# Sinkhorn attention and a gated layer on one core: a new order for the first hundred calls and the later ones, and zero products cut in pieces elsewhere

## The chip, the cores and the metric

The kernel runs on one core of a Trainium2 chip. The metric is device time in microseconds (us) of one execution, as the median of several runs; lower is better. The engines are TensorE (PE in the profile, its weight loads PEld), VectorE (DVE), ScalarE (ACT), GpSimd (POOL) and SyncE (SP, which here issues transfers).

## The reference, cut to what matters

```python
# q, k, v: 4 batches, 8 heads, 768 positions, 64 wide; sort_net: 4, 8, 8, 8
P = sort_net
for _ in range(5):                              # the balancing
    P = exp(P - max(P, -1)); P = P / sum(P, -1); P = P / sum(P, -2)
k_sorted = einsum('bhij,bhjcd->bhicd', P, k_blocks)   # 8 blocks of 96 positions
v_sorted = einsum('bhij,bhjcd->bhicd', P, v_blocks)
scores = q_block @ k_sorted_block.T / 8               # 96 x 96 for each block and head
attn = softmax(scores)
x = (attn @ v_sorted_block)                           # rearranged to 3072 tokens x 512
h = x @ w_in                                          # 512 -> 2048
out = (h * cos(h)) @ w_out                            # 2048 -> 512, float32
```

## The kernel before, in words

The 3072 tokens are worked in 8 chunks of 384 tokens. Chunk n is half of one batch: 4 tiles u of 96 positions, each with all 8 heads. A chunk passes through these calls, each a small function of the kernel that records instructions on a fixed engine:

- the sorted keys, `kp`/`ks`/`kg` (products on PE into tile `ks`) with their evictions `kpe`/`kse`/`kge` into `kTs`; the sorted values, `v0`/`vb`/`vg`/`vgT` (products into `vs`) with the evictions `v0e`/`vbe`/`vge` into `vS` or `pair`;
- `S n u` or `T n u`: the scores of a tile (tile `sc`); `M`: their row maximum on DVE (`mx`); `X`: the subtraction on DVE (`s`); `E`: the exponential on ACT (`p_buf`);
- the transposed weights, either on PE with an eviction (`TP`, tile `pps`, and `TE`, tile `pT`) or by a transposing transfer on SP's queue (`TD`);
- `AV`: weights times values on PE (`av`); `N`: a reciprocal `r` and a product `xn` on DVE;
- the transposed x, by PE and an eviction (`XP`, tile `xps`, and `XE`, tile `xT`) or by a transfer (`XD`);
- the up layer, `U` (PE, tile `h`), `C` (the cosine on ACT, tile `c`), `G` (the product on DVE, tile `gg`); for chunk 0 `U4`, `C4`, `G4` do it in halves of the tokens;
- the down layer, `D n ts q` (four products of 512 columns on PE into tile `o`), `O` (the eviction) and `W` (the write).

Which call stands where is not left to a scheduler. `PLAN` is a text of some 790 lines, one call each, and a loop at the kernel's end runs them in that order, so each engine gets its instructions in the order of the plan. Within an engine nothing overtakes. Tiles in PSUM come from two pools, `big` (three buffers; the letter B in a call) and `acc` (two buffers; the letter c); a call that needs a buffer waits until an earlier tile has been evicted. The letters A and V in an eviction say ACT or DVE. What the plan does on PE in one stretch is covered by the evictions on ACT and DVE in the next, so the chunks are interleaved: the keys and scores of chunk n+1 stand between the layers of chunk n.

The program begins with the transfers of q, k and v, the five balancing rounds (small DVE and ACT work on 32 partitions) and, beside them on PE, **zero products**: `keep_warm(times, t, cols)` (L1051 to L1062) multiplies a zero tile `warm` into a tile that is overwritten later. They are called in the balancing (tile `idle`), and inside the plan by `kp` and `v0` (as many as the last argument, 512 columns each) and by `TP` and `AV` of chunk 0 (256 columns each). A counter `pieces` allows a number of them to be cut into pieces: before, each call is cut in up to four until 70 cuts are used up, which the balancing does alone.

The balanced matrix `sorted_by` is followed on PE by `block` (tile `bl`), and on DVE by `spread` (tiles `bd` and `bdv`), which the plan's `kp` and `v0` read. `v0 3`, `v0 1`, `v0 2` and `v0 0` read v as it landed (`kv`); `v0 4` to `v0 7` read `vperm`, which `vp 32` makes from it on POOL in two copies (L993).

## Time and profile before

| what | value |
|---|---|
| median of 3 runs | 236.35 us (236.2 to 237.87) |
| the profiled execution, its own time | 236.52 us |
| its span from first to last instruction | 234.7 us |
| PE busy | 227.7 us, 97% of the span |
| DVE busy | 175.2 us, 75% |
| ACT busy | 149.1 us, 64% |
| POOL busy | 93.7 us, 40% |

The profile is of one execution; the 1.8 us between its time and its span lie around the instructions. Positions are us from the first instruction. In a timeline row stand start, duration, engine, line, operation, output and inputs, shape and count, and in brackets the idle time before it and what ended it. Products on PE are pipelined and their ends are modelled, so PE rows overlap: the time that a group costs is the distance to the start of the next. A row of the chain that ended last has start, duration and what was done; there the parts do not overlap.

### The profile page before, as it was taken

The page shows a single profiled execution, that of the slowest core. Times are in us where ns is not written, and L with a number is a line of the kernel's source. Part 1 is how long each engine was busy: PE and PEld are TensorE (multiplying, and loading weights), DVE is VectorE, ACT ScalarE, POOL GpSimd, SP SyncE. Part 2 cuts the span into 40 slices and gives each one's busy share as a digit, 9 for nine tenths or more (in the row PEclk, how much of TensorE's full clock was granted, in tenths as well). Part 3 has the DMA queues.
Part 4 walks back from the last instruction along what each step waited for, and adds up shares of the span by engine and source line. Part 5 has one row for each costly group of instructions (what it writes and reads, how often), then busy time and mean ns, then how long its engine had stood idle before and what let it go on. Part 6 is the DMA issues. An engine that isn't in the chain of part 4 may idle for free.

```text
span 234.7 us, 5734 instructions
## 1 busy us (share of the span) xinstructions
PE 227.7 (97%) x2380; PEld 151.0 (64%) x2380; DVE 175.2 (75%) x291; ACT 149.1 (64%) x198; POOL 93.7 (40%) x117
## 2 busy tenths in 40 slices
PE   8898999999999999999999999999999999999994
PEld 8766799657765566655666558655555596456553
DVE  5757987798898776897778977899487879455530
ACT  3365976657869859883788747666667376526511
POOL 7659998596990095972709000800000000000000
PEclk9999999999999999999999999999999999999999
DMA  5999999796699779996999668953943650341003
GB/s 63 223 195 207 204 207 226 128 216 164 134 102 179 167 138 168 99 218 152 127 158 95 86 104 148 210 83 68 162 159 64 82 175 3 66 125 47 0 0 134
DMA packets 66841, 31.01 MB, mean 132 GB/s; under 512 B 55552, under 2 KB 62336, under 8 KB 66560
## 3 DMA queue, kind: packets, MB, share of 16 engines
q0 software_dynamic: 24048, 13.64, 43.6%
q1 hardware_dynamic: 42480, 16.83, 34.1%
q8 instruction: 18, 0.29, 0.5%
q10 hardware_dynamic: 288, 0.20, 0.3%
q14 instruction: 7, 0.06, 0.1%
HBM read 27.27 MB, written 6.29 MB: 143 GB/s over the span
## 4 chain that ended last, share of the span: by engine, by line
PE 84%; DMA 7%; ACT 3%; POOL 3%; issue 1%; DVE 1%; DVEq 0%; POOLq 0%
PE o L1544 32%; PE h L1499 30%; DMA kv<-in_v_dram 6%; PE h L1522 5%; PE av L1430 3%; POOL vperm L993 2%; PE sc L1320 2%; PE ks L1201 2%; PE xps L1469 2%; PE o L1638 2%; DMA kv<-p_buf 1%; PE vs L1257 1%; PE pps L1406 1%; PE vs L1292 1%; PE sc L1347 1%
## 5 line engine op out<-in xcount | busy, mean ns | idle before, releaser
L1544 PE MATMUL o<-w_out_t,gg 128*128 128x512 bf16 x368 | 87.2, 379 | 0.0
L1499 PE MATMUL h<-xT,w_in_t 128*128 128x384 bf16 (+1 forms) x516 | 78.2, 305 | 0.0
L1511 DVE TENSOR_TENSOR gg<-c,h 128x768 bf16<-128x768 f32 x56 | 53.0, 949 | 19.0 <-ACT c L1505 18.9
L1505 ACT ACTIVATE c<-h,half_pi 128x768 f32<-128x768 f32 x56 | 50.4, 901 | 22.0 <-PE h L1499 20.7
L1499 PEld LDWEIGHTS <-w_in_t 128*128 128x128 bf16 x516 | 47.1, 98 | 22.4 <-DVE xT L1072 0.2
L1544 PEld LDWEIGHTS <-gg 128*128 128x128 bf16 x368 | 33.3, 98 | 33.7 <-DVE gg L1511 0.6
L1379 ACT ACTIVATE p_buf<-s 96x768 bf16<-96x768 f32 x32 | 26.4, 841 | 12.1 <-DVE s L1375 8.0
L1361 DVE TENSOR_REDUCE mx<-sc 96x8 f32<-96x768 f32 (+1 forms) x41 | 31.5, 772 | 3.3 <-PE sc L1333 1.4
L993 POOL COPY vperm<-kv 64x1536 bf16<-64x1536 bf16 (+1 forms) x10 | 28.1, 2853 | 2.5 <-DMA kv<-in_v_dram 2.5
L1375 DVE TENSOR_TENSOR s<-sc,mx 96x384 f32<-96x384 f32 (+1 forms) x33 | 24.1, 733 | 1.2
L1447 DVE TENSOR_TENSOR xn<-av,r 96x512 bf16<-96x512 f32 x32 | 22.0, 687 | 1.1
L943 POOL DMA_DIRECT2D kv<-in_q_dram x24 | 16.0, 681 | 0.8 <-issue 0.5
L1446 DVE RECIPROCAL r<-av 96x8 f32<-96x8 f32 x32 | 6.3, 198 | 8.1 <-PE av L1430 8.0
L1070 ACT CAST kTs<-ks 128x512 bf16<-128x512 f32 (+1 forms) x18 | 11.0, 632 | 2.2 <-PE ks L1201 2.2
L1070 ACT COPY xT<-xps 128x384 bf16<-128x384 bf16 x10 | 4.8, 476 | 11.3 <-PE xps L1469 11.3
L943 POOL DMA_DIRECT2D q_mem<-in_q_dram x16 | 10.7, 685 | 2.8 <-DMA kv<-in_v_dram 2.4
L1070 ACT COPY kv<-o 128x512 f32<-128x512 f32 (+2 forms) x10 | 5.3, 529 | 9.6 <-PE o L1544 7.0
L1059 PEld LDWEIGHTS <-warm 128*128 128x128 bf16 x116 | 9.8, 119 | 2.3 <-DVE half_pi L1042 1.0
L1522 PE MATMUL h<-xT,w_in_t 128*128 128x192 bf16 x128 | 11.1, 246 | 0.0
L1059 PE MATMUL idle<-warm 128*128 128x128 bf16 (+2 forms) x99 | 9.7, 273 | 1.3 <-DVE half_pi L1042 1.0
L1522 PEld LDWEIGHTS <-w_in_t 128*128 128x128 bf16 x128 | 10.4, 98 | 0.0
L1567 POOL CAST held<-q_turned 96x1 f32<-96x1 bf16 x2 | 0.4, 182 | 24.4 <-DMA q_turned<-q_mem 17.0
(120 smaller groups left out, 276.4 us busy)
## 6 DMA issues: line engine op xcount, KB each, us to landing
out_dram<-kv SPq DMA_DIRECT2D x12, 256.0 KB, 2.5
out_dram<-o_s SPq DMA_DIRECT2D x10, 256.0 KB, 3.3
w_in_t<-in_moe_w_in_dram POOLq DMA_DIRECT2D x4, 512.0 KB, 12.4
w_out_t<-in_moe_w_out_dram POOLq DMA_DIRECT2D x4, 512.0 KB, 11.6
kv<-in_k_dram POOLq DMA_DIRECT2D x2, 768.0 KB, 10.0
kv<-in_v_dram POOLq DMA_DIRECT2D x2, 768.0 KB, 13.6
pair<-in_k_dram POOLq DMA_DIRECT2D x2, 768.0 KB, 10.3
kv<-in_v_dram POOLq DMA_DIRECT2D x6, 256.0 KB, 6.1
```

The source lines that it names most:

```text
L943: nc.gpsimd.dma_start(out=q_heads[:, i, :, e], in_=src[:, ih * IC + i, :, e])
L993: nc.gpsimd.tensor_copy(dst, src)
L1070: eng.copy(dst, src)
L1361: nc.vector.reduce_max(mx[:], s_view(n, u, hp), axis=AX.XY if n < 2 else AX.X)
L1375: nc.vector.tensor_tensor(s, sc, mx.to_broadcast(list(s.shape)), op=ALU.subtract)
L1379: nc.scalar.activation(p[:, :, :blk], s_t.pop((n, u)).rearrange("p e h c -> p (e h) c"), AF.Exp, scale=scale)
L1447: nc.vector.tensor_tensor(xn.rearrange("p h e d -> p e h d")[:, e], avv[:, :, :, :D], r[:, e].to_broadcast([blk, e.stop - e.start, H2, D]) ...
L1499: nc.tensor.matmul(o[:, f2, x * w:(x + 1) * w], w_in_t[:, kk, f * 128:(f + 1) * 128], xT[n][:, kk, x * w:(x + 1) * w], start=(kk == 0), st ...
L1505: nc.scalar.activation(c[:], ps["h", n, fp][:, :, :TC], AF.Sin, bias=half_pi[:, 0:1])
L1511: nc.vector.tensor_tensor(gt[n, fp // 2][:, f:f + 2], ps.pop(("c", n, fp))[:], ps.pop(("h", n, fp))[:, :, :TC], op=ALU.mult)
L1522: nc.tensor.matmul(o[:, part, f2 * w:(f2 + 1) * w], w_in_t[:, kk, f * 128:(f + 1) * 128], xT[0][:, kk, h * w:(h + 1) * w], start=(kk == 0) ...
L1544: nc.tensor.matmul(out_ps[n, ts][:], gt[n, q][:, f % 4, ts * 128:(ts + 1) * 128], w_out_t[:, f, :], start=(f == 0), stop=(f == FC - 1))
```

## The change

Three things are changed. The plan's first hundred or so calls come in another order, and two zero products leave them (those of `kp 2` and of `v0 4`). `keep_warm` cuts differently: a product of 512 columns in up to five and one of 256 in three, 18 cuts for the balancing and 52 for the plan, of which the plan uses 44. And from chunk 0's down layer on, calls are moved by one to a few places all through the plan; `S 6 0` becomes `T 6 0` (the same scores by products of 64 rows), `U 2 6` and `U 7 6` do half of their work in products of 192 columns in place of 384, and `TE 1 3` and `vbe 4` go from DVE to ACT, `XE 2 2` from ACT to DVE.

```diff
-MORE = 70
+MORE = 18,52
 PLAN = """\
-vp 32
 kp 0 B 1
 spv
-kp 2 B 1
+kp 2 B
+kp 1 B
+vp 32
 kpe 0 A
-kp 1 B
+v0 3 c 1
+v0 4 B
+kpe 1 A
 kpe 2 V
-v0 3 c 1
-kpe 1 A
+S 0 0 B
+v0e 3 V
 v0 1 c 1
-v0e 3 V
-S 0 0 B
+v0e 4 A
+S 0 1 B
 v0e 1 A
-v0 4 B 1
...
     AV 2 1
     N 2 1
     kg 3 B
+O 1 1 o A
+X 3 0
+D 1 2 0
...
-T 4 0 B
-vge 0 8 A
-AV 3 1
 hp 3 3
 Lq 5
+T 4 0 B
 D 2 1 1
 M 4 0
 X 4 0
+AV 3 1
 N 3 1
+vge 0 8 A
...
-    pieces = [MORE]
+    pieces = [MORE[0]]
...
-            n = 1 + min(3, pieces[0])
+            n = min(1 + pieces[0], max(3, cols // 102))
...
+    pieces[0] = MORE[1]
     for line in PLAN.split("\n"):
```

After the change, lines from L1052 on have a number that is one higher. The first place is PE after the sorted keys: before, the last products of `v0 1` (from `kv`) are followed by the scores `S 0 0`.

```order
L1257 LDWEIGHTS kv
L1257 MATMUL vs<-bdv,kv 128x128
L1257 LDWEIGHTS kv
L1257 MATMUL vs<-bdv,kv 128x64
L1333 LDWEIGHTS q_turned_94
L1333 MATMUL sc<-kTs,q_turned_94 128x64
```

After the change the last products of `v0 3` are followed by `v0 4`, which reads `vperm`, and the scores come behind it.

```order
L1258 MATMUL vs<-bdv,kv 128x128
L1258 LDWEIGHTS kv
L1258 MATMUL vs<-bdv,kv 128x64
L1258 LDWEIGHTS vperm
L1258 MATMUL vs<-bdv,vperm 128x128
```

So PE's scores of tile 0 now stand behind a product that waits for POOL's first copy into `vperm`.

The second place is DVE at the end of chunk 1's down layer, where chunk 2's tiles are finished; numbers tell the tiles apart. Before, `M 3 0` and `X 3 0` (the rows with `sc_1694`) come ahead of `N 2 1` (those with `av_1713`).

```order
L1446 RECIPROCAL r_1666<-av_1650 96x8
L1447 TENSOR_TENSOR xn_1667<-av_1650,r_1666 96x2x4x64
L1361 TENSOR_REDUCE mx_1707<-sc_1694 96x8
L1375 TENSOR_TENSOR s_1709<-sc_1694,mx_1707 96x768
L1446 RECIPROCAL r_1722<-av_1713 96x8
L1447 TENSOR_TENSOR xn_1723<-av_1713,r_1722 96x2x4x64
```

After the change the same six are in this order (`sc_1683` and `av_1699` are the same two tiles).

```order
L1447 RECIPROCAL r_1661<-av_1649 96x8
L1448 TENSOR_TENSOR xn_1662<-av_1649,r_1661 96x2x4x64
L1362 TENSOR_REDUCE mx_1697<-sc_1683 96x8
L1447 RECIPROCAL r_1708<-av_1699 96x8
L1448 TENSOR_TENSOR xn_1709<-av_1699,r_1708 96x2x4x64
L1376 TENSOR_TENSOR s_1719<-sc_1683,mx_1697 96x768
```

`N 2 1` now stands ahead of `X 3 0`, one long DVE instruction earlier.

The third place is PE in chunk 2's down layer, at `T 4 0` (the last scores there are of tile `sc`) and `AV 3 1` (from `kv`, where a transfer puts the transposed weights). Before, one follows the other.

```order
L1347 MATMUL sc<-kTs,q_turned_94 128x96
L1347 LDWEIGHTS q_turned_94
L1347 MATMUL sc<-kTs,q_turned_94 128x96
L1430 LDWEIGHTS kv
L1430 MATMUL av<-vS,kv 128x65
```

After the change `D 2 1 1`, four products of 512 columns, stands between them; its last two are shown.

```order
L1545 LDWEIGHTS gg
L1545 MATMUL o<-w_out_t,gg 128x512
L1545 LDWEIGHTS gg
L1545 MATMUL o<-w_out_t,gg 128x512
L1431 LDWEIGHTS kv
L1431 MATMUL av<-vS,kv 128x65
```

`AV 3 1` thus comes four products later behind the same scores. In the same stretch `AV 3 0` and `N 3 0` moved to the stretch's beginning, so that on DVE `N 3 0` now stands ahead of `M 3 3` and `X 3 3`.

## The prediction

> **What bounds the kernel now.** I read the busy times first (the page's, then by stretches), then the waits of PE, then the chain that ended last and timelines of single stretches.

> ```profile
> PE 227.7 (97%) x2380; PEld 151.0 (64%) x2380; DVE 175.2 (75%) x291; ACT 149.1 (64%) x198; POOL 93.7 (40%) x117
> 20.00:25.00 5.00, 4.41 (x92) 3.57 (x92) 4.16 (x6) 3.92 (x7) 4.94 (x7) 1.00 1.29 203
> 180.00:200.00 20.00, 20.00 (x193) 14.23 (x191) 15.80 (x24) 11.94 (x15) 0.00 (x0) 1.00 0.45 92
> ```

> PE is busy for 97% of the span; DVE, the next, has a quarter of its time free. By stretches of the span (columns: length, then PE, PEld, DVE, ACT and POOL busy) PE has gaps early (4.41 of 5 us from 20 to 25) and none late (20.00 of 20). A new order of calls changes no amount of real work. It can only take away waits of PE, so the waits are the whole purse:

> ```profile
> PE vs L1257 <- POOL vperm L993: 0.6, 1, 0.6
> PE qps L1136 <- DMA q_mem<-in_q_dram: 0.6, 1, 0.6
> PE av L1430 <- DMA kv<-p_buf: 0.3, 1, 0.3
> PE pps L1406 <- ACT p_buf L1379: 0.2, 1, 0.2
> ```

> The wait for the queries (`q_mem`) stands in the balancing, whose order the change leaves alone, and so do the rows left out here. What remains is 0.6 for `vperm`, 0.3 for a transfer and 0.2 for an exponential, 1.1 us or 0.5% of the time, and stalls that are too short for this view. That caps a gain. A loss has no such cap.

> **The early stage.** The chain there, up to the first product of the up layer:

> ```profile
> 15.74 5.55 POOL vperm L993 x2
> 25.42 0.87 PE vs L1257 x8
> 26.32 0.58 ACT vS L1070
> 27.69 0.56 PE pps L1406 x8
> 30.87 2.68 PE h L1522 x32
> ```

> POOL copies v as soon as it has landed, PE works through values and scores until `v0 0` (25.42), whose eviction on ACT stands ahead of the exponential of tile 3, which the transposes at 27.69 wait for. The question is when `v0 0` is done in the new order. These rows of PE's and POOL's timelines give it:

> ```profile
> 17.63 0.39 PE L1059 MATMUL vs<-warm 128*128 128x512 bf16 x1
> 19.02 0.39 PE L1059 MATMUL vs<-warm 128*128 128x512 bf16 x1
> 19.34 0.59 PE L1257 MATMUL vs<-bdv,vperm 64*128 64x128 bf16 x8
> 21.34 0.20 PE L1257 MATMUL vs<-bdv,vperm 64*128 64x64 bf16 x1 [0.59 <-POOL vperm L993]
> 26.21 0.28 PE L1059 MATMUL pps<-warm 128*128 128x256 bf16 x1
> 15.74 2.78 POOL L993 COPY vperm<-kv 64x1536 bf16<-64x1536 bf16 x1 [2.10 <-DMA kv<-in_v_dram]
> ```

> From 17.63 (the zero product ahead of `v0 1`) to 26.21 (behind `v0 0`) PE takes 8.58 us. In it are the wait of 0.59 and the zero product of `v0 4`, 19.34 - 19.02 = 0.32, which goes. The new order does the same work (the `TP 0 0` that stood in its middle is still ahead of `v0 0`), but it starts with `v0 4`, which needs the first copy: 15.74 + 2.78 = 18.52, and 0.05 to see it (as 21.34 stands behind 15.74 + 5.55). Without wait and zero product the rest is 8.58 - 0.59 - 0.32 = 7.67, so `v0 0` ends at 18.57 + 7.67 = 26.24, against 26.21. The wait at 21.34 goes, and a longer one takes its place: PE now reaches `v0 4` at about 17.3 (before, `v0 3` ended at 17.63, and the 0.32 for the zero product of `kp 2` ahead of it are gone) and stands until 18.57. **This stage gives nothing.**

> The cuts add a little. Eight products of 384 columns take 1.30 us in the chain, and 32 of 192 take 2.68 (at 30.87):

> ```profile
> 88.51 1.30 PE h L1499 x8
> ```

> That is 163 ns against twice 84, so one more product costs some 5 ns. Of the 44 cuts in the plan some 24 stand behind `v0 4` and ahead of the up layer, 0.12 us; the others are covered by the wait for `vperm`. In the balancing a cut more or less is covered by the wait for the queries (the 0.6 above). The two `U` that are split add four products each, 0.04 together.

> What could make the stage better: tile 1's scores now come before `v0 5`, so DVE no longer stands between `X 0 0` and `M 0 1`:

> ```profile
> 21.81 0.95 DVE L1361 TENSOR_REDUCE mx<-sc 96x8 f32<-96x768 f32 x1 [0.74 <-PE sc L1333]
> ```

> It loses 0.3 at the start (`S 0 0` waits for POOL too) and saves the 0.74, some 0.4 us. If the DVE chain set the end of this stage, that would be the gain; by the chain above ACT behind `v0 0` sets it. I take +0.12, with -0.4 and +0.5 (`S 0 0` late by all of it, and nothing won back) as ends.

> **The DVE order at 82 us.** The chain and the timeline there:

> ```profile
> 82.72 0.95 DVE s L1375
> 83.83 0.70 DVE xn L1447
> 84.57 0.34 PE xps L1469 x4
> 85.78 0.26 PE av L1430 x8
> 84.04 0.42 PE L1430 MATMUL av<-vS,pT 96*128 96x65 bf16 x8
> ```

> PE issues `AV 2 2` at 84.04, and eight such products cost 0.26 (the row at 85.78), so it is free at 84.30; `XP 2 1` starts at 84.57 because `xn` of `N 2 1` ended at 84.53, behind `X 3 0`. With `N 2 1` ahead of `X 3 0` that ends 0.95 earlier, and `XP 2 1` waits for nothing: **-0.27**. What is late next is `X 3 0`, by 0.9 us, and behind it the exponential of tile 3 0, whose result is first used in the next down layer.

> **The wait at 107 us.** `AV 3 1` waits for its transposing transfer:

> ```profile
> 106.97 0.43 PE av L1430 x8
> 106.30 0.34 PE L1347 MATMUL sc<-kTs,q_turned 64*128 64x96 bf16 x8
> ```

> `T 4 0` starts at 106.30. Eight such products cost 0.28 behind ones of 128 rows and make the next ones 0.10 longer (both in the last fence of this part); I take 0.10 for either change of rows, and as `T 4 0` stands behind products of 64 rows it costs 0.18. So PE is ready at 106.48 and starts at 106.97. Of these 0.49 the change of rows is 0.10. With `D 2 1 1` between (0.86 us, half of the 1.73 in that fence), PE comes to `AV 3 1` at 107.44, after the landing. But another thing is late by then. `AV 3 1` takes the buffer of `vgT 0`, which ACT evicts in order behind `E 3 3`:

> ```profile
> 103.97 0.95 DVE L1375 TENSOR_TENSOR s<-sc,mx 96x768 f32<-96x768 f32 x1
> 105.07 0.69 DVE L1447 TENSOR_TENSOR xn<-av,r 96x512 bf16<-96x512 f32 x1
> 104.95 0.84 ACT L1379 ACTIVATE p_buf<-s 96x768 bf16<-96x768 f32 x1 [0.20 <-DVE s L1375]
> 105.70 1.00 ACT L1070 CAST pair<-vs 96x1024 bf16<-96x1024 f32 x1
> ```

> `N 3 0` (0.84 us, from the end of `X 3 3` at 104.92 to 105.76) now stands ahead of `M 3 3`, so `X 3 3` ends at about 105.75 in place of 104.92, `E 3 3` at 106.6, and the eviction at 107.5. PE waits 0.1 for it. I take **-0.29**, with 0 and -0.39 as ends.

> **T in place of S for tile 6 0**, at nothing:

> ```profile
> 155.16 0.39 PE sc L1320 x8
> 155.56 1.73 PE o L1544 x8
> 157.28 0.45 PE sc L1347 x16
> 157.73 1.83 PE o L1544 x8
> 151.67 0.28 PE sc L1347 x8
> ```

> Before: 0.39 + 0.45, and 0.10 more for the eight products behind the narrow ones (1.83 against 1.73), 0.94. After: sixteen narrow ones (0.45 + 0.10) and eight (0.28 + 0.10), 0.93. The evictions that change engine take 0.5 to 0.8 us of engines that are idle a quarter or a third of the span; I cost them at nothing. The other moves shift work by one place between engines that wait for PE; I cost them at nothing, and their risk stands in the second rival.

> **The sum.** 236.52 (the profiled execution's own time) + 0.12 + 0.04 - 0.27 - 0.29 + 0 = 236.1. That execution stands 0.17 above the median of the three runs, so the forecast is **235.9 us**, 0.2% below 236.35. A measurement of this kernel can tell about 1% from no change, so this is "within 1%".

> **Rivals.**

> 1. *The early stage pays after all.* If DVE sets its end, -0.4 in place of +0.12, and the whole 0.39 at 107 us: 235.9 - 0.5 - 0.1 = 235.3; with every wait of the view gone too, 234.9. For it: DVE is busy 4.16 of the 5 us from 20 to 25, nearly as much as PE (4.41). Against it: the chain, which runs over ACT. Chance 0.17.

> 2. *The waits come back elsewhere.* Where the keys and values of the next chunk stand between the up layers, PE takes a buffer just after ACT has evicted it: `kg 7`'s eviction ends at 92.75, and the scores that take its buffer start at 92.86.

> ```profile
> 92.17 0.58 ACT L1070 CAST kTs<-ks 128x512 bf16<-128x512 f32 x1
> 92.86 0.33 PE L1320 MATMUL sc<-kTs,q_turned 128*128 128x96 bf16 x4
> ```

> With 0.1 us of slack a moved call is enough for a stall; an eviction behind one cosine (0.9 us) stalls PE 0.3 to 0.8. Two such stalls give 236.4 to 237.3. Against it: most of the moves in these stretches put an eviction earlier. Chance 0.23.

> 3. *PE slows down.* The new order leaves PE idle from 17.3 to 18.57, 1.3 us, with no zero product in it. Zero products at the start show what a slow PE is:

> ```profile
> 1.00:6.00 5.00, 5.00 (x48) 1.00 0.68 79
> 6.20:6.90 0.70, 0.70 (x13) 1.00 1.13 222
> ```

> 48 in 5.00 us are 104 ns each, 13 in 0.70 are 54, at a granted clock that reads 1.00 in both. If the pause sends PE back to the slow pace for as long as at the start (5.1 us), a stage in which PE is the bound loses half of that, 2.55, and up to 3.2 if work with gaps takes longer to bring it back: 238.5 to 239.1, slower than before. It decides if a pause of 1.3 us is enough; the pause of 0.59 at 21.34 was not, for eight values behind it still cost 0.87 (25.42). Chance 0.05. [...]

> That the cuts do nothing is no rival but my term: 0.12 us. The forecast's own case, 235.3 to 236.4, has 0.55.

> **Range and chances.** From the first rival's 234.9 to the second's 237.3: the three cases inside hold 0.95, less what I leave for stalls that I have not seen. Slower by over 1% (above 238.7) is most of the third rival and larger stalls of the second, 0.06; faster by over 1% (below 234.0) would need more than the waits hold, 0.04; within 1% 0.90.

> **What the new profile would show.** Right: PE waiting some 1.2 us at `v0 4` for `vperm` at 18.5, no wait at 21.3, the up layer's first product within 0.3 us of 30.87, no gap ahead of `XP 2 1` near 84, and the wait of `av` for `kv<-p_buf` gone. Wrong: a stretch after 18.6 in which products take twice as long; a first up-layer product before 30.4; a new wait of PE of over 0.3 us behind an eviction.

## The result and the profile after

The changed kernel takes 234.83 us (median of 8 runs, 234.45 to 235.42) against 236.42 us before (8 runs beside it, 235.81 to 237.87). The ratio is 0.9928, 95% interval 0.9909 to 0.9946: 0.7% faster, where 0.2% was forecast, and just below the lower end of the range, 234.9. Ratios here and below are of runs near a kernel's fastest, medians are of all its runs. On a second occasion it took 234.87 us against 236.45, ratio 0.9935 (0.9923 to 0.9948). The profiled execution took 235.34 us, its span is 233.6 us, 1.1 less than before.

The waits of PE after (what waited, for what; us in total, times, longest):

```profile
PE sc L1348 <- DMA kTs<-kTs: 0.7, 1, 0.7
PE pps L1407 <- ACT p_buf L1380: 0.2, 1, 0.2
```

The waits for `vperm` (0.6) and for `kv<-p_buf` (0.3) are gone. A wait of 0.7 for the transfer of the swapped keys (`kTs<-kTs`, issued by the call `kswap 1`) is new. The chain that ended last, in the early stage:

```profile
23.74 0.87 PE vs L1258 x8
24.64 0.59 ACT vS L1071
26.01 0.56 PE pps L1407 x8
29.17 1.98 PE h L1523 x24
```

`v0 0` (before at 25.42) comes 1.7 us earlier, and so does the up layer (30.87 before). The timelines of POOL and PE say why:

```profile
14.31 5.54 POOL L993 COPY vperm<-kv 64x1536 bf16<-64x1536 bf16 x2 [0.77 <-DMA kv<-in_v_dram]
17.15 0.50 PE L1258 MATMUL vs<-bdv,vperm 64*128 64x128 bf16 x6
```

POOL starts its copies at 14.31, not at 15.74. The first ends at 17.07, just before PE comes to `v0 4` at 17.15: there is no pause. The two later places, on PE's timeline:

```profile
84.25 0.51 PE L1470 MATMUL xps<-order,xn 96*128 96x96 bf16 x8
105.37 0.33 PE L1348 MATMUL sc<-kTs,q_turned 64*128 64x96 bf16 x7 [0.71 <-DMA kTs<-kTs]
106.50 0.42 PE L1431 MATMUL av<-vS,kv 96*128 96x65 bf16 x8
```

`XP 2 1` has no gap ahead of it, and `AV 3 1` does not wait, but `T 4 0` now does. (Some records of products of 512 columns are missing from this trace, so its count of products on PE is too low.)

By stretches between the first products of the down layers the gain reads as follows (us, from the trace, by PE's weight loads).

| stretch | before | after | gain |
|---|---|---|---|
| to the up layer of chunk 0 | 30.72 | 28.96 | 1.76 |
| to chunk 1's down layer | 42.55 | 42.83 | -0.28 |
| to chunk 2's down layer | 27.33 | 26.97 | 0.36 |
| to chunk 3's down layer | 27.31 | 27.82 | -0.51 |
| from there to the last weight load | 103.22 | 103.35 | -0.13 |

The early stage, forecast at nothing, gives more than the whole change; the place at 107 us, forecast at a gain of 0.29, loses 0.51. The -0.28 in the second row had no term in the forecast. late_only (below), with the old early stage, takes 42.78 us there and 26.97 in the next stretch, so both of these differences belong to the later list; what costs the 0.28 was not traced.

### The profile page after: what moved, and what is told of

The parts are those of the page before. It is cut to its first block, busy times and chain, and to the rows that moved or that the text cites. A ratio compares the mean times of both kernels' runs of the same rounds, so it can differ in the third digit from the quotient of the medians.

```text
span 233.6 us, 5709 instructions
## 1 busy us (share of the span) xinstructions
PE 224.9 (96%) x2358; PEld 148.6 (64%) x2378; DVE 173.8 (74%) x290; ACT 149.9 (64%) x199; POOL 93.7 (40%) x117
## 4 chain that ended last, share of the span: by engine, by line
PE 77%; DMA 7%; ACT 4%; POOL 4%; DVE 3%; issue 2%; SPq 1%; POOLq 0%; ACTq 0%
PE o L1545 28%; PE h L1500 27%; PE h L1523 5%; DMA kv<-in_v_dram 3%; PE av L1431 3%; POOL vperm L993 2%; DMA kTs<-kTs 2%; PE vs L1258 2%; PE sc L1321 2%; PE o L1640 2%; DMA pT<-p_buf 1%; PE pps L1407 1%; PE vs L1293 1%; PE xps L1470 1%; PE ks L1202 1%
## 5 line engine op out<-in xcount | busy, mean ns | idle before, releaser
L1545 PE MATMUL o<-w_out_t,gg 128*128 128x512 bf16 x349 | 85.1, 379 | 1.1 <-issue 0.2
L1500 PEld LDWEIGHTS <-w_in_t 128*128 128x128 bf16 x524 | 47.7, 98 | 22.2 <-DVE xT L1073 0.4
L1380 ACT ACTIVATE p_buf<-s 96x768 bf16<-96x768 f32 x32 | 26.4, 841 | 12.7 <-DVE s L1376 10.3
L993 POOL COPY vperm<-kv 64x1536 bf16<-64x1536 bf16 (+1 forms) x10 | 28.1, 2848 | 3.7 <-DMA kv<-in_v_dram 3.7
L1447 DVE RECIPROCAL r<-av 96x8 f32<-96x8 f32 x32 | 6.3, 198 | 7.3 <-PE av L1431 7.1
L1060 PE MATMUL idle<-warm 128*128 128x512 bf16 (+4 forms) x46 | 9.0, 364 | 2.3 <-ACT q_turned L1143 1.2
L1060 PEld LDWEIGHTS <-warm 128*128 128x128 bf16 x106 | 7.7, 111 | 5.5 <-issue 2.8
L1071 ACT COPY xT<-xps 128x384 bf16<-128x384 bf16 x9 | 4.3, 475 | 10.3 <-PE xps L1470 10.3
L1523 PEld LDWEIGHTS <-w_in_t 128*128 128x128 bf16 x128 | 10.4, 98 | 0.1
## 6 DMA issues: line engine op xcount, KB each, us to landing
pair<-in_k_dram POOLq DMA_DIRECT2D x2, 768.0 KB, 10.9
```

Source lines behind the costliest of these rows:

```text
L993: nc.gpsimd.tensor_copy(dst, src)
L1071: eng.copy(dst, src)
L1380: nc.scalar.activation(p[:, :, :blk], s_t.pop((n, u)).rearrange("p e h c -> p (e h) c"), AF.Exp, scale=scale)
L1500: nc.tensor.matmul(o[:, f2, x * w:(x + 1) * w], w_in_t[:, kk, f * 128:(f + 1) * 128], xT[n][:, kk, x * w:(x + 1) * w], start=(kk == 0), st ...
L1523: nc.tensor.matmul(o[:, part, f2 * w:(f2 + 1) * w], w_in_t[:, kk, f * 128:(f + 1) * 128], xT[0][:, kk, h * w:(h + 1) * w], start=(kk == 0) ...
L1545: nc.tensor.matmul(out_ps[n, ts][:], gt[n, q][:, f % 4, ts * 128:(ts + 1) * 128], w_out_t[:, f, :], start=(f == 0), stop=(f == FC - 1))
```

## The experiments

v was issued at the same time in both (2.74 and 2.73 us), by the same instructions. The first question was why it landed 1.4 us earlier: by the change (theory A, of which theory F below is the mechanism), by chance (B), or whether the gain is the later list's anyway (C).

| kernel | median us | runs | ratio (95%) | runs with mean clock under 0.98 |
|---|---|---|---|---|
| pieces_only | 236.36 | 12 | 0.9989 (0.9976 to 1.0003) | 0 |
| early_only | 242.42 | 12 | 0.9957 (0.9934 to 0.998) | 8 |
| late_only | 237.09 | 12 | 1.0027 (1.0005 to 1.005) | 0 |
| early_pieces | 235.32 | 12 | 0.9959 (0.9931 to 0.9986) | 0 |
| all_70 | 244.45 | 6 | none | 5 |
| early_18 | 238.28 | 11 | 1.0064 (1.0041 to 1.0088) | 1 |
| early_fill | 236.16 | 12 | 0.998 (0.9962 to 0.9998) | 0 |
| all_T40 | 234.60 | 6 | 0.9926 (0.9913 to 0.994) | 0 |
| all_idle | 243.73 | 5 | 1.0296 (1.0275 to 1.0317) | 5 |
| all_18_0 | 236.72 | 12 | 1.0025 (0.9999 to 1.0052) | 0 |
| all_T40_S | 235.55 | 5 | 0.996 (0.9948 to 0.9972) | 0 |
| fetch_134 | 234.76 | 5 | 0.9928 (0.9914 to 0.9941) | 0 |
| fetch_131 | 237.11 | 10 | 1.0032 (1.0017 to 1.0046) | 0 |

The last column counts runs in which the clock was halved for a good part of the early stage (below). Besides, seven runs of early_18, four of all_18_0 and one of early_pieces show a mean clock of 0.993. The kernel before stayed at 0.997 or more in all 88 runs beside these. fetch_7 (one run) and after_again stand in the text.

### One part alone

**pieces_only**

```diff
-MORE = 70
+MORE = 18,52
-    pieces = [MORE]
+    pieces = [MORE[0]]
-            n = 1 + min(3, pieces[0])
+            n = min(1 + pieces[0], max(3, cols // 102))
```

> The kernel before with the new rule for the zero products alone (18 cuts in the balancing, 52 for the plan), old order everywhere. Theory A (the new rule brings the values in earlier: with other counts of instructions in the balancing the transfer of v lands near 14.3 us in place of 15.7): v lands near 14.3, the wait at v0 4 shrinks, the up layer starts near 30.0 and the time is 0.5 to 0.8 us below before. Theory B (the landing of v varies by itself, and the gain is the order's): v lands anywhere from 14 to 16, and the time is within 0.3 us of before. Theory C (the later list gives the gain): no difference from before.

Its transfers up to 16 us (KB each, median us from issue to landing), and then those of before:

```profile
kv<-in_k_dram POOLq DMA_DIRECT2D x1, 768.0 KB, 8.1
kv<-in_v_dram POOLq DMA_DIRECT2D x1, 768.0 KB, 11.4
```

```profile
kv<-in_k_dram POOLq DMA_DIRECT2D x1, 768.0 KB, 8.7
kv<-in_v_dram POOLq DMA_DIRECT2D x1, 768.0 KB, 12.9
```

v lands at 14.16, 3.83 us behind k (before 4.82 behind it). So the new rule for the zero products moves v. The up layer starts 0.57 earlier, which is the wait for `vperm`; but `T 4 0` waits 0.3 us for `kTs`, `AV 3 1` 0.4, and nothing is left at the end. A holds for the landing, its time does not.

**early_only**: the plan after up to `U4 0 2 0`, the rest as before.

```diff
-vp 32
 kp 0 B 1
 spv
-kp 2 B 1
+kp 2 B
+kp 1 B
+vp 32
...
+v0 4 B
```

> The kernel before with the new order up to U4 0 2 0 (two zero products fewer), old rule for the zero products and old list behind it. Theory A: v lands near 15.7 as before, PE waits about 1.2 us ahead of v0 4, the up layer starts within 0.3 us of 30.75, and the time is within 0.3 us of before. Theory B: the time that the stage takes follows the landing of v; with a landing at 14.3 the up layer starts near 29.0 and the time is 1.2 to 1.7 us below before, with a landing at 15.7 nothing is gained. Theory C: no difference from before.

The page's granted clock in 40 slices (tenths):

```profile
PEclk9995557999999999999999999999999999999999
```

PE's wait:

```profile
PE vs L1257 <- POOL vperm L993: 1.3, 1, 1.3
```

Three stretches (length, busy us of PE, PEld, DVE, ACT, POOL, then the granted clock, the DMA share and GB/s):

```profile
17.20:18.60 1.40, 0.09 (x3) 0.01 (x1) 0.69 (x1) 0.00 (x0) 1.40 (x2) 1.00 1.23 204
18.80:39.20 20.40, 20.40 (x232) 17.22 (x230) 12.74 (x20) 11.10 (x16) 19.22 (x24) 0.50 1.25 211
39.30:44.00 4.70, 4.70 (x63) 4.66 (x62) 2.55 (x5) 3.07 (x4) 1.71 (x6) 1.00 0.79 166
```

This is the pause that I forecast for the change, with v at 15.71 and PE standing from 17.28 to 18.59. What follows is not my likeliest case but my third rival: the clock reads 0.50 from 18.74 to 39.22, the up layer starts at 37.59, and that run takes 244.67 us. Eight of twelve runs take 241.05 to 244.67; the other four 235.56 to 235.86. None of the theories A to C had foreseen it.

**late_only**: the plan after from `U4 0 2 1` on, the rest as before (the first moved calls as diff).

```diff
+QP 1 0 B
 C4 0 2
 U4 1 0 1
+C4 1 0
+D 0 0 0
 G4 0 2
-QP 1 0 B
-C4 1 0
```

> The kernel before with the new list from U4 0 2 1 on (chunk 0's down layer and all behind it), old order and old rule ahead of it. Its first 40 us are the program before, so the landing of v in its profile is one more sample of the same program: theory A wants 15.5 to 15.9, theory B anything from 14 to 16. Theories A and B: time within 0.4 us of before (my sum had -0.5 for this part, of which the new wait of T 4 0 for the transfer of the keys takes some back). Theory C: 1.2 to 1.7 us below before.

v lands at 15.51, 5.12 us behind k: one more sample of the old early stage. The time is 0.3% above before. The profile, of the slowest of the twelve runs (238.16 us), shows a wait at 136 us that the old list does not have:

```profile
PE av L1430 <- DMA kv<-p_buf: 1.2, 1, 1.2
```

C is out. The later list by itself gains nothing.

**early_pieces**: both diffs of pieces_only and early_only.

> The new order up to U4 0 2 0 and the new rule for the zero products, with the old list behind it. Theory A: all of the early gain, v near 14.3, up layer from about 29.0, time 1.2 to 1.7 us below before, and less than the whole change loses later. Theory B: the time of early_only, within 0.3 us, whatever the zero products. Theory C: no difference from before.

v lands at 14.12, 3.83 us behind k, the up layer starts at 28.96, and the time is 0.9959 of before: 0.4%, somewhat under what A expected. The whole change is at 0.9928 and 0.9935, so the later list seems to be worth some 0.3% here, though the intervals overlap; beside the old early stage it lost 0.3%. The parts do not add up.

### What moves v, and what halves the clock

The page has a queue q8 of kind "instruction", with 18 packets of 16,384 bytes. I read them as PE's instructions: PE has some 4,760 products and weight loads, so one packet for about every 250, and the packets move with their number (below). The first such packet of a profile takes 0.89 to 1.04 us of one of the 16 DMA engines, later ones up to 1.8 us. The queue in short stretches, before from 11.5 to 12.6 us and after from 13.9 to 15 (packets, MB, share of the 16 engines' time):

```profile
q8 instruction: 1, 0.02, 5.4%
```

```profile
q8 instruction: 1, 0.02, 5.5%
```

Before, PE's first fetch starts at 11.62, while v is coming in; after, at 13.98, when v's last packet has ended (13.74). k and v come in 128 packets of 12,288 bytes, 0.93 us each. Spread evenly, v is by my estimate four packets on each engine, 3.7 us; the engine that carries the fetch has a fifth. This is theory F. (The trace does not name the engine of a packet; that the fetch shares one with v is read from the landing.) It was tested by the number of cuts alone:

**all_70**

```diff
-MORE = 18,52
+MORE = 70,52
```

> The whole change, but the balancing may use 70 cuts as before in place of 18 (the plan keeps its 52). Theory F (more PE instructions in the balancing bring PE's instruction fetch into the transfer of v and delay it) with theory P (a pause of 1.3 us ahead of v0 4 halves the clock for some 20 us): v lands near 15.7 us, PE waits 1.2 to 1.3 us at v0 4, the granted clock falls to 0.50 and the time is 240 to 244 us in most runs. F without P: v near 15.7, clock 1.00, time 235.3 to 236.2. Rival to F (the landing has to do with something else in the change): v near 14.3 and the time of the whole change, 234.5 to 235.4.

The fetch starts at 11.44 and v lands at 15.10, 4.80 us behind k. PE waits for `vperm`:

```profile
PE vs L1258 <- POOL vperm L993: 0.7, 1, 0.7
```

The clock falls at 17.94; the 13.65 us ahead of that:

```profile
4.29:17.94 13.65, 10.99 (x209) 8.37 (x207) 9.14 (x34) 5.69 (x10) 9.75 (x13) 1.00 1.14 208
```

Five of six runs took 242.40 to 247.63 us. F holds, and the rival to it is out. **So with the balancing's cuts of before, the new order would have been some 3% slower in most runs** (the sixth took 238.19). The pause was 0.7 us, less than the 1.2 that P named.

**early_18**: early_only with one number changed.

```diff
-MORE = 70
+MORE = 18
```

> The kernel early_only with one number changed: 18 cuts in the balancing in place of 70, by the old rule, and none in the plan. Theories F and P: PE's fetch falls behind the transfer of v, v lands near 14.2 us, PE waits less than 0.2 us at v0 4, no run shows a clock of 0.96, and the time is 235.0 to 235.5 us, as early_pieces or 0.1 less (44 products fewer). Rival to F: v near 15.7 and most runs at 241 to 244 us as in early_only. Rival to P (the clock falls because zero products are missing): runs at 241 to 244 us although v lands early.

The fetch starts at 13.98, v lands 3.80 us behind k, PE waits 0.3 for `vperm`: F holds. P does not: in the profiled run (245.13 us) the clock falls at 17.97 although the pause is short. That run's PE had stood 1.6 us for the queries and 0.5 for a copy before. The other runs took 236.34 to 238.84, where 235.0 to 235.5 was expected; seven of them have a mean clock of 0.993, which I estimate at 3.3 us at half clock (twice 0.7% of 236.6 us, their span). `T 4 0` waits 1.6 us for `kTs`, of which more below.

**early_fill**: early_only with zero products in the pause.

```diff
-v0 4 B
+v0 4 B 4
```

> The kernel early_only with four zero products of 512 columns ahead of v0 4 (0.85 us of PE's work inside the pause of 1.3 us), nothing else changed. Theory P: v lands near 15.7 us as in early_only, the pause shrinks to about 0.45 us, the clock stays at 1.00 in all runs, and the time is 235.5 to 236.2 us. Rival (the clock falls for another reason than the pause): most runs at 241 to 244 us as in early_only.

PE's timeline at `v0 4`:

```profile
17.23 1.04 PE L1059 MATMUL vs<-warm 128*128 128x512 bf16 x4
18.20 0.51 PE L1257 MATMUL vs<-bdv,vperm 64*128 64x128 bf16 x6
```

The stretch that was slow in early_only:

```profile
18.80:39.20 20.40, 20.21 (x331) 18.04 (x324) 17.56 (x27) 16.32 (x23) 19.77 (x27) 1.00 1.25 211
```

v still lands late (15.12, 4.84 us behind k), PE has something to do, and the clock is 1.00 in all twelve runs. Time: 0.2% below before. **This is the early stage that I had forecast**: late values, little gain, and a full clock. It needed zero products that the change does not have. Its up layer starts at 29.91, 0.84 earlier than before; 0.57 of that is v, which lands at 15.12 and not at 15.69.

Is it then the pause at `v0 4`, or PE's idle time in all? The times between changes of the clock are multiples of 3.41 us here: it was at 0.50 for 20.48 us in early_only (six steps) and 17.07 in all_70 (five), and in both it fell 13.65 us (four steps) after PE had come to full pace.

**all_idle**

```diff
-                idle((6, 2)[it - 2])
+                idle((1, 2)[it - 2])
```

> The whole change with five zero products fewer in the balancing (one in place of six behind the second round), 1.07 us of PE's work; nothing waits for them. In the change's profile PE idles 0.90, 0.48, 0.51 and 0.00 us in the four windows of 3.41 us that follow the change to the full clock, 1.89 in all; this kernel should have 2.9 to 3.0, with nothing in the fourth. Theory S (the clock is halved where PE's idle time over the first 13.65 us at full clock comes to more than some 2.1 to 2.5 us, wherever it lies): the clock falls to 0.50 near 18 to 19.5 us though PE does not wait at v0 4, and most runs take 237 to 245 us. Rival (it takes a pause at v0 4, just ahead of the fall, or some idle time in each of the four windows): clock 1.00 and 234.4 to 235.4 us, as the whole change.

```profile
4.59:11.42 6.83, 4.30 (x60) 2.15 (x59) 5.07 (x21) 2.12 (x5) 4.94 (x8) 1.00 1.17 227
11.42:18.24 6.82, 6.42 (x90) 4.73 (x89) 2.75 (x10) 2.63 (x4) 5.79 (x5) 0.50 1.11 194
```

All five runs took 242.61 to 245.35 us, with five zero products fewer that nothing waits for. The clock fell already at 11.41, after two steps with 2.53 us idle, long before `v0 4`. So the fall did not take that pause, and S was right that idle time at other places can do it; the fall came sooner than S had it. The 13.65 us to the fall in early_only and early_18, and the same length in two kernels in which it did not fall there:

```profile
5.09:18.74 13.65, 10.69 (x204) 8.53 (x202) 8.55 (x30) 5.70 (x10) 9.15 (x13) 1.00 1.14 212
```

```profile
4.32:17.97 13.65, 11.11 (x169) 6.82 (x168) 9.18 (x33) 5.70 (x10) 10.15 (x13) 1.00 1.14 208
```

```profile
5.26:18.91 13.65, 11.76 (x203) 8.17 (x203) 9.27 (x31) 6.28 (x11) 10.67 (x12) 1.00 1.14 211
```

```profile
4.29:17.94 13.65, 11.27 (x193) 7.47 (x193) 9.14 (x34) 5.87 (x11) 10.65 (x13) 1.00 1.14 208
```

PE busy 10.69, 10.99 (all_70) and 11.11 us: it falls. 11.76 (the changed kernel) and 11.27 (all_T40_S): it does not, nor in fetch_131 with 11.18. That would set the point near 2.5 us of idle time, but all_18_0 was busy for 11.09 of the 13.65 us up to 109.22 and kept its clock in that run, and fetch_7 lost it at 108.47 after 1.94 us idle in one step. What exactly is counted stays open.

### The fetch elsewhere

**all_18_0**

```diff
-MORE = 18,52
+MORE = 18,0
```

> The whole change with no cuts in the plan (18 in the balancing, 44 products fewer behind it). By my term a cut costs 5 ns, so 24 of them ahead of the up layer cost 0.12 us: the up layer starts 0.1 us earlier and the time is 0 to 0.2 us below the whole change, 234.5 to 234.9. Rival (the cuts are worth something, by where PE's later instruction fetches fall or by the clock): 235.2 us or more.

The up layer starts at 28.88, 0.12 earlier, as my 5 ns a cut had it. Yet the median is 1.9 us above the whole change. Four of the twelve runs (238.18 to 238.96) have the mean clock of 0.993; the other eight, at a full clock, have a median of 236.2, still 1.4 above. PE's timeline at `T 4 0` (in a run at full clock):

```profile
106.89 0.33 PE L1348 MATMUL sc<-kTs,q_turned 64*128 64x96 bf16 x7 [2.36 <-DMA kTs<-kTs]
```

The second transfer of the keys (L1247) is issued twice in the program, and the longest of these rows is the one that `T 4 0` waits for, first here and then in the changed kernel:

```profile
DMA to landing us min/median/max: 3.0/4.9/6.8
```

```profile
DMA to landing us min/median/max: 4.1/4.8/5.6
```

With 44 products fewer, PE's fetch of 98.27 comes at 103.95, in that transfer, and the keys land 6.8 us after their issue in place of 5.6. The rival was right: the cuts are worth something, by where they put the fetches.

**fetch_7**: the kernel before, with finer cuts at the start.

```diff
-MORE = 70
+MORE = 105
-            n = 1 + min(3, pieces[0])
+            n = 1 + min(7, pieces[0])
```

> The kernel before with the first fifteen zero products cut in eight in place of four (105 cuts in place of 70), so that PE's first instruction fetch comes near 7 us, in the transfer of k, and its second near 15.9, behind v. Theory F (the 16 KB of a fetch take 0.9 us of one of the DMA engines, and what is in flight on it lands that much later): the fetch is seen near 7 us, k lands 0.7 to 1.2 us later than the 10.3 to 10.9 of the other runs, and v lands 3.6 to 4.1 us behind k, not 4.8 to 5.1. Rival (v lands late because of the number of zero products): v 4.8 us or more behind k, and k at 10.3 to 10.9.

```profile
kv<-in_k_dram POOLq DMA_DIRECT2D x1, 768.0 KB, 9.6
kv<-in_v_dram POOLq DMA_DIRECT2D x1, 768.0 KB, 12.9
```

The fetch came at 8.82, later than meant but in the transfer of k. k landed at 11.75, 0.8 to 1.5 later than elsewhere, and v 3.87 us behind it. F holds; more zero products do not by themselves widen the distance. (The run took 244.14 us: its later fetches fell into two transposing transfers, on which PE waited 2.2 and 1.6 us, and its clock stood at 0.50 for 6.83 us.)

Over all profiles, with the start of a fetch (us) beside what landed:

| what | fetch inside it | fetch elsewhere |
|---|---|---|
| v behind k | 4.80 to 5.12 us in 5 profiles (fetch at 10.59 to 11.62) | 3.74 to 3.93 in 12 |
| second key transfer of `kswap 1` behind the first | 2.82 to 3.00 in 3 (all_70, early_18, all_18_0) | 1.73 to 2.03 in 14 |
| second transfer of chunk 4's `xT` behind the first | 2.62 to 3.49 in 11 | 1.33 to 1.36 in 5 |

Left out of the last row is fetch_134, in which the fetch hit the first of the two. No profile lies on the wrong side. By these ranges a fetch inside a transfer delayed its landing by 0.9 to 1.4 us for v, 0.8 to 1.3 for the keys and 1.3 to 2.2 for `xT`.

**all_T40**: work put into the new wait at 105 us.

```diff
-T 4 0 B
 D 2 1 1
+T 4 0 B
 M 4 0
 X 4 0
+D 2 2 0
 AV 3 1
 N 3 1
 vge 0 8 A
-D 2 2 0
```

> The whole change with two calls moved: D 2 1 1 ahead of T 4 0, and D 2 2 0 ahead of AV 3 1. Theory K (0.87 us are given back at T 4 0, which waits for the transfer of kswap 1 held up on SP behind QD 4): PE does D 2 1 1 while the transfer lands, T 4 0 starts near 105.4 as now without a wait, and the time is 0.4 to 0.8 us below the whole change, 234.0 to 234.5. Rival (what is saved there is lost at the next transfer, TD 3 1 for AV 3 1 or TD 3 2): the wait moves to AV 3 1 or AV 3 2 and the time is within 0.2 us of the whole change.

PE's timeline there, and below it the longest of its waits behind the early stage:

```profile
105.49 0.34 PE L1348 MATMUL sc<-kTs,q_turned 64*128 64x96 bf16 x8
106.64 0.42 PE L1431 MATMUL av<-vS,kv 96*128 96x65 bf16 x8
```

```profile
PE h L1500 <- DMA xT<-xn: 0.4, 1, 0.4
```

The wait for the keys is gone, and chunk 3's down layer starts 0.7 us earlier than in the changed kernel; at 139 us PE waits for `xT`, whose transfer holds a fetch (135.90). In the end 0.4 us are left in the profile (span 233.2 against 233.6), and the ratio cannot be told from the changed kernel's. Both theories were half right.

**all_T40_S**: scores in the place of that wait.

```diff
+S 5 2 c 0
 U 4 1 1
 C 4 1
 O 3 2 v V
 O 3 1 v A
 U 4 2 2
 C 4 2
 G 4 1
-S 5 2 c 0
```

> all_T40 with S 5 2 c 0 ahead of U 4 1 1, so that PE has 0.2 to 0.3 us of other work while the transfer for xT lands, for which it waited 0.4 us at 139.24. Theory K: the wait shrinks to 0.2 us or less and the time is 0.1 to 0.4 us below all_T40, 234.2 to 234.5. Rival (the transfers behind it set the pace, and the time comes back at the next one): within 0.1 us of all_T40's 234.6.

A miss: the scores take a buffer that DVE has not yet emptied, 0.8 us of waiting, and 235.55 us.

```profile
PE sc L1321 <- DVE kv L1073: 0.8, 1, 0.8
```

**fetch_134** and **fetch_131** move the fetch itself, by products added 15 to 25 us ahead of it:

```diff
-U 3 0
+U 3 0 2
-U 3 1
+U 3 1 2
```

> all_T40 with U 3 0 and U 3 1 done in products of 192 columns in place of 384 (16 products and 16 weight loads more, 0.08 us of PE). In all_T40 PE's fetch at 135.90 lies in the last transfer for xT, which lands at 139.11 and holds PE for 0.43 us. Theory F: 32 instructions more bring that fetch to 134.5, ahead of that transfer, which then lands 1.3 us behind the one before it in place of 3.5; the wait ahead of the up layer at 139.2 goes, and the time is 0.2 to 0.5 us below all_T40's 234.6 although PE has more to do. Rival (the cuts and splits only cost): 234.6 to 234.8 with the wait as it was.

> all_T40 with U 3 0 to U 3 5 done in products of 192 columns (48 products and 48 weight loads more, 0.24 us of PE). Theory F: 96 instructions more bring the same fetch to about 131.4, into the transposing transfer for AV 4 0, which in all_T40 lands at 132.26 with 0.1 us to spare; it lands about 1 us later, PE waits 0.8 to 1.2 us at AV 4 0, and the time is 0.5 to 1.2 us above all_T40. Rival (the cuts and splits only cost): 0.2 us above all_T40, 234.8, with no wait at AV 4 0.

In fetch_134 the fetch starts at 135.11, the second `xT` lands 0.50 us behind the first, the wait at 139 is gone, and at 150 us PE is 0.38 ahead of all_T40. At 182.7 PE waits for a transfer that did not hold it in all_T40 (PE's fetch there has moved from 182.32 to 180.87), and the gain is lost:

```profile
PE av L1431 <- DMA vperm<-p_buf: 0.2, 1, 0.2
```

In fetch_131 (`U 3 0` to `U 3 5`) the fetch starts at 130.66, and PE waits at `AV 4 0` as meant, though 0.5 us and not 0.8 to 1.2. Its timeline there, and a further wait, at 181 us:

```profile
133.38 0.43 PE L1431 MATMUL av<-pair,kv 96*128 96x65 bf16 x8 [0.51 <-DMA kv<-p_buf]
```

```profile
PE av L1431 <- DMA vperm<-p_buf: 0.7, 1, 0.7
```

The loss is 2.5 us, not 0.5 to 1.2. F holds at the place that was aimed at; neither total came out as expected. Every fetch behind it moves too; that this is the rest of the loss was not shown.

**after_again**: the changed kernel a second time.

> The changed kernel again, beside the two others on one chip. Theories F and S: v lands 3.7 to 3.9 us behind k, the clock stays at 1.00, time 234.4 to 235.4 us. That the landing was chance: v 4.8 us or more behind k, or a fall of the clock.

v lands 3.87 us behind k, the clock is full, and the time is 234.87 us. `T 4 0` waits only 0.3 there; SP issued the first of the two key transfers 1.35 us earlier, and the second 0.63.

## Why the prediction was wrong

**The early stage** was the wrong term: nothing forecast, 1.76 us gained. The step that failed is "15.74 + 2.78 = 18.52": I took the landing of v as given. Behind it stands the sentence that in the balancing a cut more or less is covered by the wait for the queries. As PE's time that is so. But the 52 cuts that leave the balancing are 104 instructions of PE, and these moved its first fetch from 11.62 to 13.98, out of v's transfer. With the measured 17.15 in place of 18.57 my own 7.67 gives 24.82 for the end of `v0 0`; it was 24.53. Of these 0.29 some 0.17 is the wait at 21.34, which I took at 0.59: `v0 5` and the scores behind it take 1.51 us before (20.18 to 21.69) and 0.75 after (19.63 to 20.38), 0.76 less. So 1.42 of the stage's 1.76 is the landing, and "this stage gives nothing" was some 0.3 short even with late values. Neither part gives the gain alone: early values in the old order bring the up layer 0.57 forward (pieces_only), both together 1.79 (early_pieces). That early_fill came to the -0.2% of the forecast is chance, for it has the old later list. Nor is the order with late values settled: the four runs of early_only at full clock are 0.4% below before, and no trace of them was kept.

**The first rival** (the early stage pays after all, 0.17) named the nearest times, 235.3 and 234.9, but not for its reason, that DVE sets the end. The chain after runs over `v0 0` and its eviction on ACT, as before; what came earlier was v. Had I leaned to this rival, it would have been luck.

**The third rival** (a slow PE) had 0.05, my estimate. For the change as it is, it did not come true. For the change as I thought it to be, with v at 15.7, it came in 8 of 12 runs (early_only) and in 5 of 6 with the whole new list (all_70). It was judged by the length of one pause; in all_idle 2.53 us of idle time, spread over several places, did it. Its price was too low as well: I took the 5.1 us of slow pace at the start and a loss of 2.55 to 3.2 us (that work with gaps brings the pace back later, for the 3.2, no run shows), but in early_only's profile the clock stayed at 0.50 for 20.48 us, and the eight runs took 5 to 9 us more than the other four. The clock fell with at most 1.1 us (all_70) to 1.9 (fetch_7) idle in any one step of 3.41 us, and in early_only it stayed at 0.50 for six steps although PE was busy for all of the 20.40 us from 18.80 to 39.20.

**The cuts** at 5 ns each: right as PE's time (0.12 us, all_18_0), wrong as their whole effect, 1.4 us the other way at a full clock.

**`XP 2 1`**: 0.27 forecast; the stretch is 0.36 shorter than before, and 0.29 shorter than in early_pieces, which has the old list there. Right.

**`AV 3 1`**: its wait went, as forecast, but what is late next was not ACT's eviction. It was the keys' transfer for `T 4 0`, which SP issues behind `QD 4`; before, that call had 0.1 us to spare. The term is +0.51 in place of -0.29 (in after_again the stretch is 0.07 shorter than before, with a wait of 0.3). The second rival's "waits come back elsewhere" is right in kind, though behind a transfer and not behind an eviction.

The signs named: no wait at 21.3, no gap near 84 and no wait for `kv<-p_buf` came true; the 1.2 us at `v0 4` did not, and "a first up-layer product before 30.4" was named as a sign of error, and it is at 29.00: the sign of error came.

## What to carry to other kernels

## What the runs showed of the hardware

- One fetch of 16 KB in a 768 KB load (64 packets, 16 engines) delayed its landing by 0.9 to 1.4 us (5 profiles against 12); at three places of the program the landings fall into two groups with nothing between them.
- In four profiles (early_only, all_70, early_18, all_idle) the granted clock fell to 0.50 with 2.5 to 3.0 us of idle time in the first 7 to 14 us at full pace, and stayed there for five to seven steps of 3.41 us. One and the same kernel (early_only) took 235.6 to 235.9 or 241.1 to 244.7 us.
- With 44 products of zeros fewer, 0.12 us of PE's time ahead of the up layer, the kernel was 1.4 us slower at a full clock (all_18_0).
